# Causal mask of the first two token blocks: from one VectorE product to a ScalarE copy and a GpSimd select

## The chip, the cores and the metric

One core of a Trainium2 chip runs the whole program; the other cores do nothing. The metric is the time of one execution on the device in microseconds (us), and lower is better. Three executions of the kernel before gave 1217.30, 1218.65 and 1219.31 us, so the median is 1218.65 us.

The engines go by short names: PE is the matrix engine (PEld its weight loads), DVE is VectorE, ACT is ScalarE, POOL is GpSimd, and SP is the engine that issues most of the transfers. Each works through its own list of instructions in a fixed order.

## The reference

A gated linear recurrence (4 batches, 8 heads, 768 tokens, 48 channels) feeds two gated feed-forward layers of 3072 tokens, the second with a normalisation ahead of it:

```
a = (a_re + i a_im) * min(|a|, 0.999) / (|a| + 1e-6)
for t in range(S):
    S_state = a[t] * S_state + outer(k[t], v[t])        # complex state, 48 x 48 per head
    y[t]    = q[t] @ real(S_state)
x   = y as [3072, 384]
x   = (silu(x @ w_gate) * (x @ w_val)) @ w_out          # layer 1
out = the same with other weights on rmsnorm(x)         # layer 2
```

## The kernel before

**The recurrence** is computed in six blocks of 128 tokens. Within a block, q is multiplied by the running product of the decays and k is divided by it, so that the contribution of token p to token t is an ordinary dot product of the two. That product (`score`, PE, L699) gives for each head a 128 x 512 tile `sp` in PSUM: a row is a key token p, and the columns are four batches of 128 query tokens. Only pairs with t not before p may count. So `sp` is multiplied with a mask tile that holds -1 where t is not before p and 0 elsewhere (built once at the start, L309 to L314). The minus is there because k arrives negated from the Newton step at L653. The product (L703, DVE) writes the SBUF tile `pt`, and PE multiplies `pt` with v (`yy`, L716). From the second block on, q times the state of the earlier blocks is added (L721).

**A group** is two heads of one block, with all four batches, so there are four groups to a block and 24 in all. For each group PE transposes k and q (`trans`, L684, tile `tp`), ACT copies them to SBUF (L690 for k, L687 for q, tile `T`), PE makes the scores, DVE masks them, PE makes `yp`, and ACT copies it out (L723, tile `yt`). The update of the state (`zz`, L740, L742, then L747 to L750 on DVE) of a group is put among the instructions of the next group. What the transposes need comes from DVE and ACT: decays and their running products for two groups at a time (`e1`, L474 to L502, and `scan`), then per group a square (L618), a sum (L621), a logarithm and an exponential (L626, L627), a Newton step (L652, L653), and the products `qt` and `kt` (L646, L655, L659).

**The first layer** follows block by block: a block's feed-forward (`gv`, L360; `silu`, L369; product, L378; `acc`, L792) runs while the recurrence of the next block is computed. Its weights are split into two halves on the way in, 36 pieces in all: a transfer of 3 to 4 us, three DVE operations (L59 to L61), three ACT operations with accumulators (L330 to L332), two matmuls (`wl`, L335, L336) and another ACT copy (L337). All of that lies in the first 250 us. The second layer has no recurrence beside it.

**What sets the order.** `in_order` sorts the pieces of all tasks by due times from tables, and that is the order in which the program is written. A scheduler in the framework then orders each engine's list by priorities and its own estimates of when things are ready, so an edit in one place can move instructions elsewhere. PSUM holds two tiles under the tag `at`, which `tp`, `sp`, `yp` and `zp` share in turn; `pt` has two SBUF buffers.

**ACT's tables.** Silu needs one table of functions, logarithm and exponential share another, and each change is an instruction of its own, ACT_TABLE_LOAD. `both_logs` (L419) asks for the shared table ahead of the logarithms (L420). Where a Silu stands between that load and a logarithm, the logarithm gets a load of its own, under its own line.

Of the kernel before, what the change touches and what calls it, by code (L numbers as in the profile page):

```python
# [13 lines left out]
AF = mybir.ActivationFunctionType  # L14
ALU = mybir.AluOpType
# [3 lines left out]
B, H, S, D = 4, 8, 768, 48  # L19
# [3 lines left out]
R = 32  # L23
# [23 lines left out]
LOPE = (1, 1)  # L47
G2 = 2
NFE = G2 * D
NB = 2 * NFE // 32  # L50


LOW = 2.0 ** -15 * 1.125  # the upper word of 2^-126, read as a float


def narrow(V, raw, y):
    """float64 words -> y, the same number with float32's 24 bits."""
    lo, hi, yu = raw[:, :, 0], raw[:, :, 1], y.bitcast(U32)
    V.tensor_scalar(yu, hi, 3, 0x3FFFFFF8, op0=ALU.logical_shift_left, op1=ALU.bitwise_and)  # L59
    V.scalar_tensor_tensor(yu, hi, 0xC0000000, yu, op0=ALU.bitwise_and, op1=ALU.bitwise_or)  # L60
    V.scalar_tensor_tensor(yu, lo, 29, yu, op0=ALU.logical_shift_right, op1=ALU.bitwise_or)  # L61


def words(w, f, out_rows):
    """Block f of 128 hidden units of a weight, as [128, 768] words (or floats)."""
    k = 2 if w.dtype == U32 else 1
    if out_rows:
        return w[f * 128:f * 128 + 128, :]
    return w[:, k * f * 128:k * (f * 128 + 128)].rearrange("(c p) f -> p c f", p=128)
# [12 lines left out]


def in_order(tasks, wires):
    """The items of all tasks by the time they are due, each after those it is wired to."""
    due, after, need = {}, {}, {}
    for t, (name, (start, dur, items)) in enumerate(tasks.items()):
        total, acc = sum(c for c, _ in items), 0.0
        for n, (c, _) in enumerate(items):
            due[name, n] = (start + dur * (acc + 0.5 * c) / total, t, n)  # L90
            acc += c
            need[name, n] = 1 if n else 0
            if n:
                after.setdefault((name, n - 1), []).append((name, n))
    for a, b in wires:
        after.setdefault(a, []).append(b)
        need[b] += 1
    heap = [(due[x], x) for x in due if need[x] == 0]
    heapq.heapify(heap)
    out = []  # L100
    while heap:
        _, x = heapq.heappop(heap)
        out.append(tasks[x[0]][2][x[1]])
        for y in after.get(x, ()):
            need[y] -= 1
            if need[y] == 0:
                heapq.heappush(heap, (due[y], y))
    assert len(out) == len(due)
    return out
# [2 lines left out]
@with_exitstack  # L112
def plain_path(ctx: ExitStack, tc: tile.TileContext, q, k, v, a_re, a_im,
               wg, wv, wo, w2g, w2v, w2o, rms_g, out):
    """The recurrence step by step: for decays that a chunk's running product cannot carry."""
    nc = tc.nc
    V, A, T, SY = nc.vector, nc.scalar, nc.tensor, nc.sync
    TB, EG = 16, 4
# [6 lines left out]
    with tc.tile_pool(name="pl1", bufs=1) as p1, tc.tile_pool(name="pl2", bufs=2) as p2:  # L125
# [4 lines left out]
        with tc.For_i(0, S // TB, 1) as blk:  # L130
# [35 lines left out]
            z = [p1.tile([128, E, D], F32, name=f"pl_z{n}") for n in range(3)]  # L166
# [14 lines left out]
    with tc.tile_pool(name="pw", bufs=1) as pw, tc.tile_pool(name="px", bufs=2) as px, \  # L181
# [6 lines left out]
        for n, (g_, v_, o_) in enumerate(((wg, wv, wo), (w2g, w2v, w2o))):  # L188
# [3 lines left out]
            for f in range(NF):  # L192
                for x, t in ((g_, tg), (v_, tv), (o_, to)):
                    x = words(x, f, x is o_)
# [67 lines left out]
def decay_attention_two_ffn(ctx: ExitStack, tc: tile.TileContext, q, k, v, a_re, a_im,  # L262
# [25 lines left out]
    with ExitStack() as fast:  # L288
# [24 lines left out]
                            pattern=[[1, u], [u, R]], channel_multiplier=-1)  # L313
            masks[u] = m  # L314

# [1 line left out]
        def load_w(w, srcs, f, layer, which=(0, 1, 2)):  # L317
            for i in which:
                x = srcs[i]
# [25 lines left out]
        PAIRS = ((0, 0), (0, 1), (1, 0))  # L345

        def ffn_items(W, x, N, acc_mm, done):
            """One block of a gated layer: W[f] -> weights, x = (hi, lo) getter."""
            items = []
            st = {}  # L350

# [49 lines left out]
            items.append((0.01, done))  # L401
            return items

# [1 line left out]
        att = ExitStack()  # L405
        ap1 = att.enter_context(tc.tile_pool(name="ap1", bufs=1))
        ap2 = att.enter_context(tc.tile_pool(name="ap2", bufs=2))
# [42 lines left out]
            vt[i] = t  # L450

        def cmul(dst, t1, t2, pr, pi, z):
            """dst = (pr + i pi) * z with dst, z, t1, t2 stacked [128, 2, ...]."""
            V.tensor_tensor(t1, pr, z, op=ALU.mult)
            V.tensor_tensor(t2, pi, z, op=ALU.mult)
            V.tensor_tensor(dst[:, 0], t1[:, 0], t2[:, 1], op=ALU.subtract)
            V.tensor_tensor(dst[:, 1], t1[:, 1], t2[:, 0], op=ALU.add)

        def stack(z, like):
            """A real tile [128, ...] against a stacked one."""  # L460
            return z[:, None].to_broadcast(list(like.shape))

        def e1(p):
            """Decays of four heads, and their running products over the u tokens of a row."""
            gr = groups[2 * p]
            U, n = gr.blk.U, 2 * gr.blk.el
            s = {}
# [52 lines left out]
            return items  # L520

        def scan(p):
            """Running products over the 32 rows of a quadrant, for four heads."""
            gr = groups[2 * p]
            blk0 = gr.h0 * D // 32
            P = carry[:, :, blk0:blk0 + NB]
# [48 lines left out]
            return [(1, tr), (1.5, first), (2, pairs)] + [(2, hs(d)) for d in (1, 2, 4, 8)] + [(2, fill), (1, newcarry)]  # L575

        def back(p):
            """Products up to each row, back to tokens."""
            gr = groups[2 * p]
            U, el = gr.blk.U, gr.blk.el  # L580
            s = {}

            def go():
                x = xs[p]
                s["Xt"] = ap1.tile([128, 2, 2 * NFE], F32, tag="Xt", name="Xt", bufs=BUFS["Xt"])
                V.transpose(s["Xt"].rearrange("p c f -> p (c f)"), x[:, :, :, 0:32].rearrange("p c n r -> p (c n) r"))
                xl = an[p][:, :, U - 1]
                for c in range(2):
                    V.transpose(xl[:, c], x[:, c, :, 1:33])
                ab = ap1.tile([128, 2, 2 * NFE], F32, tag="sc1", name="ab")  # L590
                A.activation(ab, xl, AF.Abs)
                md = ap2.tile([128, 2 * G2, 2, D], F32, tag="md", name="md", bufs=BUFS["md"])
                bc = lambda z: z.rearrange("p (g d) -> p g d", d=D)[:, :, None, :].to_broadcast([128, 2 * G2, 2, D])
                V.tensor_tensor(md, bc(ab[:, 0]), bc(ab[:, 1]), op=ALU.add)
                mt[p] = md
            return s, [(3, go)]
# [76 lines left out]
        def pe_att(i):  # L673
# [21 lines left out]
            def score(h):  # L695
                def go():
# [2 lines left out]
                        T.matmul(ps[:C, bb * C:bb * C + C], o[h, 1][:, bb], o[h, 0][:, :, bb, :], start=True, stop=True)  # L699
                    t = ap2.tile([128, 512], F32, tag="pt", name="pt", bufs=BUFS["pt"])  # L700
                    m = masks[U].rearrange("p u r -> p (u r)")[:, None, :].to_broadcast([C, B, C])
                    with tc.high_priority(HP_AT):
                        V.tensor_tensor(t[:C, :N].rearrange("p (b c) -> p b c", b=B),  # L703
                                        ps[:C, :N].rearrange("p (b c) -> p b c", b=B), m, op=ALU.mult)
# [61 lines left out]
                return go  # L766
            return [(1.2, at(x)) for x in range(6)]

# [1 line left out]
        W1 = {}  # L770

        def split_x(blk):
# [84 lines left out]
        for _, fn in in_order(sch, wires):  # L857
            fn()

# [1 line left out]
        W2 = {}  # L861

        def norm(c0):
# [22 lines left out]
            return xh, xl  # L886

        def rows_of(c0, c1):
            """Columns c0:c1 of x1d as runs (partition, row of the output, length)."""
            runs = []  # L890
            for blk in blocks:
                for bb in range(B):
# [38 lines left out]
        G.memset(ones, 1.0)  # L931
        wx = fast.enter_context(tc.tile_pool(name="wx", bufs=EARLY))
        nb_ = NT // 512
        # weights of the second layer follow the last use of the first's
        def w2_loader(f):
            def go():
                W2[f] = (wx if f < EARLY else wpool).tile([128, 2, 9, 128], F32R, tag="w", name="w")
# [25 lines left out]
                    x2[n + 1] = norm(512 * (n + 1))  # L963
                fn()

# [1 line left out]
    with tc.tile_pool(name="fl", bufs=1) as fl_, tc.tile_pool(name="fps", bufs=1, space=PSUM) as fps:  # L967
        with tc.manual_schedule():
            V.tensor_scalar(stat[:, 0], stat[:, 0], 1e18, None, op0=ALU.is_le)
# [48 lines left out]
```

## Time and profile before

| what | value |
|---|---|
| median of three executions | 1218.65 us (1217.30 to 1219.31) |
| span of the profiled execution, first to last instruction | 1218.1 us (its own time is not given beyond that) |
| PE busy | 1136.6 us, 93% |
| DVE busy | 772.5 us, 63% |
| ACT busy | 668.2 us, 55% |
| POOL busy | 1.5 us, 12 instructions |
| mask products on DVE (L703) | 48, of which 16 in the first two blocks |

The busy shares are means over parts with different limits, so the windows matter more than the table. A useful ruler in this kernel is the copy of `yp` (L723), one per group: its starts cut the beginning of the run into stages. They are at 62.83, 79.37, 100.68 and 114.88 us for the four groups of the first block, and at 167.19, 195.50, 226.07 and 253.00 us for the second block. Stage 1 ends at the first of these, stage 8 at the last.

### The profile page before, as it was taken

How to read it: one execution, taken by the hardware profiler on the slowest of the kernel's cores; microseconds unless marked ns; L12 is line 12 of the kernel's file. 1: busy time of each engine (PE TensorE's matmuls, PEld its weight loads, DVE VectorE, ACT ScalarE, POOL GpSimd, SP SyncE). 2: the span in 40 equal slices, each digit the busy share in tenths (PEclk: the TensorE clock that was granted, in tenths of full speed). 3: DMA queues.
4: the chain of work that ended last, by engine and by line, in shares of the span. 5: the costliest groups of instructions: out<-in, count | busy, mean ns of one | idle time of the engine just before them, and what ended most of it. 6: DMA issues, size and time to landing. Idle time of an engine off the chain costs nothing.

```text
span 1218.1 us, 16677 instructions
## 1 busy us (share of the span) xinstructions
PE 1136.6 (93%) x6098; PEld 945.7 (78%) x6098; DVE 772.5 (63%) x1703; ACT 668.2 (55%) x1159; POOL 1.5 (0%) x12
## 2 busy tenths in 40 slices
PE   2368979999999999999999999999999999999997
PEld 1256767788888888888878887888888888888886
DVE  5997989989898696888754488742422424224222
ACT  5666979877677656675464688742421424214211
POOL 0000000000000000000000000000000000000000
PEclk9877989999999999999999999999999999999999
DMA  6355454432423224232313244400010000000000
GB/s 166 87 138 145 120 151 124 141 110 74 107 77 101 72 63 119 57 85 67 98 59 97 79 130 145 128 26 27 1 52 1 26 26 1 26 1 1 27 1 29
DMA packets 105514, 90.84 MB, mean 75 GB/s; under 512 B 34000, under 2 KB 92368, under 8 KB 105424
## 3 DMA queue, kind: packets, MB, share of 16 engines
q1 hardware_dynamic: 102832, 84.97, 24.8%
q10 hardware_dynamic: 2592, 4.72, 1.0%
q8 instruction: 50, 0.82, 0.3%
q14 instruction: 40, 0.33, 0.1%
HBM read 66.06 MB, written 18.87 MB: 70 GB/s over the span
## 4 chain that ended last, share of the span: by engine, by line
PE 72%; ACT 11%; DVE 8%; DMA 5%; issue 1%; SPq 1%; ACTq 0%; DVEq 0%
PE gv L360 39%; PE o L912 12%; PE acc L792 8%; PE sp L699 4%; PE tp L684 3%; DMA wraw<-in_moe_w_gate_dram 2%; ACT T L690 2%; PE zp L740 2%; PE yp L716 2%; DMA wraw<-in_moe_w_val_dram 2%; PE yp L721 1%; ACT w L331 1%; ACT L420 1%; ACT T L687 1%; ACT w L332 1%
## 5 line engine op out<-in xcount | busy, mean ns | idle before, releaser
L360 PE MATMUL gv<-xh,w 128*128 128x512 f32 x1728 | 571.4, 396 | 0.3 <-ACT h L369 0.3
L360 PEld LDWEIGHTS gv<-xh,w 128*128 128x128 f32 x1728 | 324.6, 188 | 68.7 <-issue 2.1
L360 PE MATMUL gv<-xl,w 128*128 128x512 f32 x864 | 339.5, 393 | 0.0
L378 DVE TENSOR_TENSOR gv<-h,gv 128x512 f32<-128x512 f32 x144 | 99.8, 693 | 225.5 <-PE gv L360 219.5
L369 ACT ACTIVATE h<-gv 128x512 f32<-128x512 f32 x144 | 85.7, 595 | 187.3 <-PE gv L360 186.8
L360 PEld LDWEIGHTS gv<-xl,w 128*128 128x128 f32 x864 | 162.6, 188 | 32.4 <-issue 1.7
L379 ACT ACTIVATE hh<-gv 128x512 fp32r<-128x512 f32 x144 | 85.5, 594 | 166.4 <-DVE gv L378 166.2
L387 DVE TENSOR_TENSOR hl<-gv,hh 128x512 fp32r<-128x512 f32 x144 | 99.1, 688 | 102.3 <-PE o L912 72.5
L792 PE MATMUL acc<-hh,w 128*128 128x512 f32 x432 | 149.0, 399 | 2.4 <-ACT hh L379 2.4
L912 PE MATMUL o<-w,hh 128*128 128x384 f32 x576 | 146.4, 336 | 0.2 <-ACT x1s L798 0.2
L912 PEld LDWEIGHTS o<-w,hh 128*128 128x128 f32 x576 | 105.6, 188 | 5.7 <-ACT x1s L798 0.5
L912 PE MATMUL o<-w,hl 128*128 128x384 f32 x288 | 96.9, 340 | 0.5 <-DVE hl L387 0.5
L792 PEld LDWEIGHTS acc<-hh,w 128*128 128x128 f32 x432 | 80.3, 188 | 21.3 <-ACT hh L379 4.3
L792 PE MATMUL acc<-hl,w 128*128 128x512 f32 x216 | 86.3, 399 | 0.7 <-DVE hl L387 0.7
L335 PE MATMUL wl<-wy,ident 128*128 128x384 f32 x72 | 39.1, 632 | 43.7 <-DVE wy L61 31.5
L690 ACT ACTIVATE T<-tp 96x512 f32<-96x512 f32 x48 | 52.6, 1097 | 43.0 <-PE tp L684 42.6
L699 PEld LDWEIGHTS sp<-T,T 96*128 96x128 f32 x384 | 51.0, 202 | 24.1 <-ACT T L687 22.6
L699 PE MATMUL sp<-T,T 96*128 96x128 f32 x384 | 56.9, 294 | 11.0 <-ACT T L687 10.7
L912 PEld LDWEIGHTS o<-w,hl 128*128 128x128 f32 x288 | 53.6, 188 | 2.6 <-DVE hl L387 2.6
L335 PEld LDWEIGHTS wl<-wy,ident 128*128 128x128 f32 x72 | 14.2, 228 | 51.8 <-DVE wy L61 36.4
L369 ACT ACT_TABLE_LOAD x38 | 48.8, 1283 | 3.4 <-PE gv L360 2.7
L792 PEld LDWEIGHTS acc<-hl,w 128*128 128x128 f32 x216 | 40.6, 188 | 11.1 <-DVE hl L387 2.8
(131 smaller groups left out, 1496.4 us busy)
## 6 DMA issues: line engine op xcount, KB each, us to landing
wraw<-in_moe_w_gate_dram SPq DMA_DIRECT2D x24, 384.0 KB, 3.5
wraw<-in_moe_w_val_dram SPq DMA_DIRECT2D x24, 384.0 KB, 3.5
wraw<-in_moe_w_out_dram SPq DMA_DIRECT2D x24, 384.0 KB, 3.1
kd<-kt SPq DMA_DIRECT2D x24, 384.0 KB, 2.6
ktok<-kd SPq DMA_DIRECT2D x24, 384.0 KB, 3.5
aar<-in_a_re_dram SPq DMA_DIRECT2D x48, 96.0 KB, 2.3
aar<-in_a_im_dram SPq DMA_DIRECT2D x48, 96.0 KB, 2.6
qk<-in_q_dram SPq DMA_DIRECT2D x96, 48.0 KB, 2.4
```

Of the source, the lines that this page charges most:

```text
L335: T.matmul(ps[:, :384], ident, y, start=True, stop=False)
L360: T.matmul(ps[:, :N], w[:, a, i + c, :], x()[b][:, c, :N], start=(n == 0), stop=(n == 8))
L369: A.activation(h[:, :N], st[f, 0][:, :N], AF.Silu)
L378: V.tensor_tensor(t[:, :N], st[f, "h"][:, :N], st[f, 3][:, :N], op=ALU.mult)
L379: A.activation(hh[:, :N], t[:, :N], AF.Copy)
L387: V.tensor_tensor(hl[:, :N], st[f, "t"][:, :N], st[f, "hh"][:, :N].bitcast(F32), op=ALU.subtract)
L684: T.transpose(ps[0:96, u * 128:u * 128 + 128], s[:, u, h].rearrange("p c d -> p (c d)"), ident)
L690: A.activation(t[:, :N].rearrange("p (b r u) -> p u b r", u=U, b=B), ps[0:96, :N].rearrange("p (u b r) -> p u b r", u=U, b=B), AF.Copy)
L699: T.matmul(ps[:C, bb * C:bb * C + C], o[h, 1][:, bb], o[h, 0][:, :, bb, :], start=True, stop=True)
L716: T.matmul(dst, vt[i][:C, col:col + 64], o[h, "p"][:C, bb * C:bb * C + C].rearrange("p (u r) -> p u r", u=U), start=True, stop=not inter)
L792: T.matmul(acc[e][:, :N], w[:, a, 6 + e, :], hs_[c][:, :N], start=(f == 0 and n == 0), stop=(f == NF - 1 and n == 2))
L912: T.matmul(acc[m][:, :DM], hs_[c][:, m * 128:m * 128 + 128], w[:, a, 6:9, :].rearrange("p c e -> p (c e)"), start=(f == 0 and x == 0), sto ...
```

## The change

For the first two blocks (`b.j < 2`, 16 of the 48 score tiles) the DVE product with the mask is not made. ACT copies the score tile out of PSUM with a factor of -1, and POOL then works in place on the SBUF tile: it keeps an element where (query token) - (key token) is not negative and writes 0 elsewhere. The other four blocks are as before. The diff also takes comments and docstrings out, so line numbers in the kernel after are one higher than before up to the score function and nine higher behind it.

```diff
+GMASK = 2
...
                     t = ap2.tile([128, 512], F32, tag="pt", name="pt", bufs=BUFS["pt"])
                     m = masks[U].rearrange("p u r -> p (u r)")[:, None, :].to_broadcast([C, B, C])
+                    if b.j < GMASK:
+                        A.activation(t[:C, :N], ps[:C, :N], AF.Copy, scale=-1.0)
+                        G.affine_select(out=t[:C, :N].rearrange("p (b u r) -> p b u r", b=B, u=U),
+                                        in_=t[:C, :N].rearrange("p (b u r) -> p b u r", b=B, u=U),
+                                        compare_op=ALU.is_ge, fill=0.0, base=0,
+                                        pattern=[[0, B], [1, U], [U, R]], channel_multiplier=-1)
+                        o[h, "p"] = t
+                        return
                     with tc.high_priority(HP_AT):
                         V.tensor_tensor(t[:C, :N].rearrange("p (b c) -> p b c", b=B),
                                         ps[:C, :N].rearrange("p (b c) -> p b c", b=B), m, op=ALU.mult)
```

The scheduler also moves other instructions. Apart from the masks, PE and SP hold the same instructions as before in another order, DVE's list has 32 products left instead of 48, POOL's has 16 selects more, and ACT's has 16 copies and seven table loads more (95 loads over the whole list, 88 before; four in each belong to the fallback path that isn't run). Counted between the copies L723, the stages 5 to 8 hold 4, 3, 4 and 3 loads before, and 5, 6, 7 and 3 after; all other stages have as many as before.

**ACT, the first group of the first block, second head.** Before, the three steps for the next group's k (L618, L626, L627) stand ahead of the copy of `yp`:

```order
L690 ACTIVATE T_418<-tp 96x4x128
L687 ACTIVATE T_445<-tp 96x512
L618 ACTIVATE e2t<-an 128x768
L626 ACTIVATE e2t<-e2t 128x384
L627 ACTIVATE e2t<-e2t 128x384
L723 ACTIVATE yt<-yp 128x512
```

The same place in the kernel after (L704 is the new copy, L732 the copy of `yp`, L619, L627 and L628 the three steps):

```order
L691 ACTIVATE T_419<-tp 96x4x128
L688 ACTIVATE T_446<-tp 96x512
L704 ACTIVATE pt<-sp 128x512
L619 ACTIVATE e2t<-an 128x768
L732 ACTIVATE yt<-yp 128x512
L627 ACTIVATE e2t<-e2t 128x384
L628 ACTIVATE e2t<-e2t 128x384
```

The new copy stands ahead of the square, and the logarithm and exponential now stand behind the copy of `yp`.

**ACT, the second group of the second block (stage 6), where the decays of two groups get their logarithm and exponential (L483, L484).** Before, the table load for them comes a few rows ahead (not shown), and the load for the Silu comes behind both:

```order
L483 ACTIVATE an<-an 128x768
L331 ACTIVATE w,wstat<-wraw 128x384
L484 ACTIVATE an<-an 128x768
L332 ACTIVATE w,wstat<-w,small 128x384
L337 ACTIVATE w<-wl 128x384
L488 ACTIVATE e1w,stat<-an 128x768
L570 ACTIVATE sc_1699<-X 128x2x6
L331 ACTIVATE w,wstat<-wraw 128x384
L369 ACT_TABLE_LOAD
L369 ACTIVATE h<-gv 128x512
```

In the kernel after:

```order
L421 ACT_TABLE_LOAD
L370 ACT_TABLE_LOAD
L370 ACTIVATE h<-gv 128x512
L484 ACT_TABLE_LOAD
L484 ACTIVATE an<-an 128x768
L380 ACTIVATE hh<-gv 128x512
L485 ACT_TABLE_LOAD
L485 ACTIVATE an<-an 128x768
L732 ACTIVATE yt<-yp 128x512
```

A Silu (L370) has moved in between the shared load and the logarithm, so that the load at L421 serves nothing, and logarithm and exponential have a load each; the copy of `yp` comes behind all four. The same pattern stands once more in the stage that follows, with L627 and L628.

**PE, between the first and the second group of the second block.** Before, the last `acc` of the piece ahead is followed at once by the transposes of the next group:

```order
L792 MATMUL acc_1060<-hh,w 128x512
L684 MATMUL tp<-ident,kt 96x128 x4
L684 MATMUL tp<-ident,qt 96x128 x3
L335 MATMUL wl<-wy,ident 128x384
L336 MATMUL wl<-w,neg 128x384
L684 MATMUL tp<-ident,qt 96x128
L360 MATMUL gv<-xh,w 128x512
L360 MATMUL gv<-xl,w 128x512
L360 MATMUL gv<-xh,w 128x512 x2
```

In the kernel after:

```order
L801 MATMUL acc_1068<-hh,w 128x512
L336 MATMUL wl<-wy,ident 128x384
L361 MATMUL gv<-xh,w 128x512
L361 MATMUL gv<-xl,w 128x512
L337 MATMUL wl<-w,neg 128x384
L361 MATMUL gv<-xh,w 128x512 x2
L361 MATMUL gv<-xl,w 128x512
L361 MATMUL gv<-xh,w 128x512 x2
L361 MATMUL gv<-xl,w 128x512
L361 MATMUL gv<-xh,w 128x512
L685 MATMUL tp<-ident,kt 96x128 x4
```

Nine matmuls of the feed-forward (one `gv` tile) and a weight piece, which in the kernel before are run ahead of the first group's `yp` or behind the transposes of the second, now stand between the two groups. Up to the end of each later group the number of `gv` matmuls is the same in both lists (126, 171 and 216 for the second to the fourth group of the second block).

## Rows read from the trace of the kernel before

**Rows 1.** The page: busy time of each engine, then DVE and ACT by slice.
```profile
PE 1136.6 (93%) x6098; PEld 945.7 (78%) x6098; DVE 772.5 (63%) x1703; ACT 668.2 (55%) x1159; POOL 1.5 (0%) x12
...
DVE  5997989989898696888754488742422424224222
ACT  5666979877677656675464688742421424214211
```
**Rows 2.** Windows by stage: length, then busy PE, PEld, DVE, ACT, POOL; PEclk; DMA.
```profile
30.00:62.83 32.83, 13.53 (x55) 9.13 (x54) 31.83 (x85) 19.87 (x41) 0.00 (x0) 0.82 0.29 85
62.83:79.37 16.54, 11.31 (x74) 9.29 (x74) 14.24 (x49) 9.17 (x19) 0.00 (x0) 0.73 0.48 131
79.37:100.68 21.31, 15.45 (x80) 10.58 (x80) 18.80 (x40) 16.29 (x39) 0.00 (x0) 0.72 0.60 166
100.68:114.88 14.20, 11.54 (x73) 9.27 (x74) 9.81 (x18) 9.87 (x21) 0.00 (x0) 0.69 0.33 96
114.88:167.19 52.31, 48.97 (x255) 38.00 (x253) 48.72 (x126) 44.88 (x101) 0.00 (x0) 1.00 0.50 140
167.19:195.50 28.31, 21.94 (x131) 17.31 (x132) 25.54 (x76) 20.87 (x40) 0.00 (x0) 0.88 0.47 129
195.50:226.07 30.57, 29.29 (x172) 22.59 (x172) 28.95 (x61) 28.33 (x59) 0.00 (x0) 1.00 0.57 164
226.07:253.00 26.93, 26.33 (x162) 20.98 (x163) 24.67 (x72) 19.70 (x33) 0.00 (x0) 1.00 0.34 93
253.00:640.00 387.00, 382.94 (x2431) 317.67 (x2430) 314.22 (x744) 252.28 (x348) 0.00 (x0) 1.00 0.31 84
```
**Rows 3.** Line L703: ns min/median/max, first and last start; DVE's idle time before it.
```profile
L703 DVE TENSOR_TENSOR pt<-sp,mask x48: 670/690/692, 55.9 to 637.2; 128x512 f32<-128x512 f32 x48
...
  PE sp L699: 20.8, 24
```
**Rows 4.** ACT's groups from 0 to 340 us: busy, mean ns, idle time before.
```profile
L420 ACT ACT_TABLE_LOAD x14 | 18.0, 1283 | 0.2
L369 ACT ACT_TABLE_LOAD x13 | 16.7, 1283 | 0.2
...
L723 ACT ACTIVATE yt<-yp 128x512 f32<-128x512 f32 x12 | 7.1, 592 | 14.9 <-PE yp L716 7.5 <-PE yp L721 7.4
```
**Rows 5.** POOL's selects over the whole run, by group.
```profile
L312 POOL TENSOR_SCALAR_AFFINE_SELECT mask<-mask 128x128 f32<-128x128 f32 x1 | 0.3, 313 | 0.0
...
L306 POOL TENSOR_SCALAR_AFFINE_SELECT small<-small 128x4 f32<-128x4 f32 x1 | 0.2, 194 | 0.0
```
**Rows 6.** ACT's timeline (start, length, idle before), first group of the first block.
```profile
56.80 0.83 ACT L618 ACTIVATE e2t<-an 128x768 f32<-128x768 f32 x1
58.26 0.52 ACT L626 ACTIVATE e2t<-e2t 128x384 f32<-128x384 f32 x1 [0.62 <-DVE e2t L621]
...
62.83 0.60 ACT L723 ACTIVATE yt<-yp 128x512 f32<-128x512 f32 x1 [3.49 <-PE yp L716]
```
**Rows 7.** DVE's timeline at the same place: what the exponential feeds.
```profile
61.80 0.55 DVE L652 TENSOR_TENSOR e2t<-e2t 128x384 f32<-128x384 f32 x1
```
**Rows 8.** ACT's timeline between the first two groups of the second block.
```profile
167.19 0.60 ACT L723 ACTIVATE yt<-yp 128x512 f32<-128x512 f32 x1 [2.46 <-PE yp L721]
167.81 1.28 ACT L420 ACT_TABLE_LOAD   x1
169.10 0.52 ACT L626 ACTIVATE e2t<-e2t 128x384 f32<-128x384 f32 x1
169.66 0.52 ACT L627 ACTIVATE e2t<-e2t 128x384 f32<-128x384 f32 x1
175.99 1.10 ACT L690 ACTIVATE T<-tp 96x512 f32<-96x512 f32 x1 [5.81 <-PE tp L684]
```
**Rows 9.** PE's timeline at the same place: the transposes that ended that wait.
```profile
174.90 1.06 PE L684 MATMUL tp<-ident,kt 128*96 128x128 f32 x4 [5.91 <-DVE X L457]
```
**Rows 10.** The chain that ended last, one piece of it.
```profile
423.23 2.08 PE gv L360 x9
```
**Rows 11.** The page, DMA issues: KB each, median us to landing.
```profile
qk<-in_q_dram SPq DMA_DIRECT2D x96, 48.0 KB, 2.4
```

## The prediction

> **What bounds the kernel now.** I read the page's busy line first: PE 93%, DVE 63%, ACT 55%, POOL 1.5 us in all [rows 1]. Over the whole span PE is the engine to beat, but the slices of DVE and ACT show that the load sits at the start: DVE is at seven to nine tenths from the second slice to the twelfth (some 365 us), and ACT is highest, at seven to nine tenths, from the fifth to the tenth [rows 1]. So I cut the start into stages at the copies of `yp` and read each stage's row [rows 2]. From 253 to 640 us PE is busy 382.94 of 387.00 us: there, a shift of the start is handed on to the end, and at most 4.06 us could be caught up. The change touches blocks 1 and 2, that is, everything up to 253 us. The time after is therefore the time before plus the shift of the last `yp` copy of block 2, as far as PE's order up to each group holds the same work, which the lists of both kernels show from stage 6 on.
>
> In stages 1 to 4 PE is far from full and DVE leads (31.83 of 32.83 us in stage 1), with ACT close in stage 3 (16.29 of 21.31). In stages 5 to 8 no engine leads alone: stage 5 has PE 48.97, DVE 48.72 and ACT 44.88 of 52.31; stage 7 has PE 29.29, DVE 28.95 and ACT 28.33 of 30.57 [rows 2]. Stage 6 has room, since PE and ACT both wait almost 6 us there for the k of the next group [rows 8, 9]. Stage 7 has none on any engine, and that decides my forecast.
>
> **The change, part by part.** The order shows that the change does what it says (16 products fewer on DVE, 16 copies and 16 selects more), so that is no rival.
>
> *Removed from DVE:* 16 products of 0.69 us, 11.0 us in all [rows 3]. DVE also stood 20.8 us idle ahead of 24 of the 48 products until the scores came; a third of it, 6.9 us, is an estimate for these 16. In two heads per stage that makes 1.4 us of work.
>
> *Added to ACT:* 16 copies of a 128 x 512 PSUM tile at 0.59 us, the price of the `yp` copy of the same shape [rows 4]: 9.5 us, 1.2 us a stage. What waits behind one in ACT's list is the list itself: weight pieces, the next group's `T` copies, the Silu. The scheduler has mostly put 1 to 3 us of other ACT work between the `T` copy and this one, so ACT seldom stops for PE's scores; the price is that `pt` comes later than the scores.
>
> *Added to POOL:* 16 selects. The trace has 0.313 us for 128 columns and 0.194 us for 4 [rows 5]. A line through both gives 0.68 us for 512 columns; four times the first gives 1.25 us. I take 0.7 us, nearer to a longer run of the same loop. POOL does nothing else, so only the path counts: from scores to `pt` it is 0.59 + 0.7 = 1.3 us (up to 1.84) in place of 0.69 us, and it is PE's `yp` that waits. From the second group on, PE has the state products, and partly feed-forward work, to do meanwhile; I put the cost of this at 0.5 us in stage 8, where in the list a table load and a Silu stand ahead of the copy, and at nothing in the others.
>
> *Table loads:* seven more, at 1.28 us [rows 4], 9.0 us in all: one in stage 5, three each in stages 6 and 7. What a load costs the chain is seen at 167.81 us: the logarithm behind it starts 1.29 us later [rows 8].
>
> The Trainium skill (ScalarE: Activation LUTs, What ACT_TABLE_LOAD costs) counts another 1.38 us of drain for each change of the set, 2.66 us together. By it seven loads would be an estimated 18.6 us. The 1.29 us from start to start does not show that drain, so the sum keeps 1.28.
>
> *Moved on SP:* the same transfers with some loads of q, k and the decays earlier or later. I cost that at nothing: the DMA engines are at most 0.60 busy in any of these stages [rows 2]. If that cover failed, one late load of q or k would cost its 2.4 us [rows 11].
>
> Now the stages.
>
> *Stages 1 to 4* (to 114.88 us). For DVE, eight products are gone, 5.5 us, against which stands an order that makes ACT later: the square at 56.80 must now wait for the second head's scores, and logarithm and exponential, which began at 58.26, come behind the `yp` copy that starts at 62.83 [rows 6]. With 0.6 us for that copy and 1.0 us for the two, the Newton step at 61.80 [rows 7] could begin at 64.4, 2.6 us later; two products fewer in DVE's queue give back 1.4. Stage 3, where ACT is loaded, gets 1.2 us. I take +1.0, with bounds of -5.5 (DVE alone decides) and +3.8 (2.6 + 1.2).
>
> *Stage 5.* DVE loses 1.4 us, and PE one `gv` tile of nine matmuls, 2.1 us [rows 10], which moves into stage 6; ACT's work is about as before (one load and two copies more, one weight piece and one Silu fewer). I take -1.5; bounds -2.1 and +1.3 (the load).
>
> *Stage 6.* ACT gets 3.85 us for the loads and 1.2 us for the copies: 20.87 + 5.0 = 25.9 of 28.31 us. It fits, since the list now puts a weight piece, a load and a Silu into the 5.81 us for which ACT sat waiting [rows 8], and PE runs its moved tile in the 5.91 us of its own wait [rows 9]. I take +0.5; bounds -2.1 and +3.
>
> *Stage 7.* ACT has 28.33 us of work in 30.57. Three loads (3.85), two copies (1.2), and one square and one more decay step against a weight step that leaves (0.8 on balance) make 34.2 us. ACT works in order, so without a single wait the stage is 3.6 us longer; with the 2.2 us for which it waited before, 5.8. I take +4.0.
>
> *Stage 8.* ACT goes from 19.70 to some 23 of 26.93 us, so PE with 26.33 stays the bound. +0.5 for the later `pt`; up to +2.
>
> The sum is 1.0 - 1.5 + 0.5 + 4.0 + 0.5 = **+4.5 us**. Against the profiled span of 1218.1 us that is 1222.6; the median lies 0.55 us above this span, and I carry that over: **1223.2 us**.
>
> **The rivals.**
>
> *A, DVE's relief decides (faster).* Place: the stages in which DVE is over 90% busy. DVE gives up 11.0 us of work and an estimated 6.9 us of waiting, and ACT's extra 18.5 us fall into its idle time, of which stages 5 to 8 hold 24.3 us and stages 1 to 4 another 30 [rows 2]. PE is idle for 11.6 us in stages 5 to 8, and more than that can't be won there; half of the 11.0 us is a fair price, -5, so 1213.6 us. It decides if the first feed-forward matmul comes earlier by more than what stage 7 loses, that is, by 4 us or more. Against it: ACT's sum for stage 7 exceeds the stage, and idle time in other stages doesn't help there.
>
> *B, a balance.* The loads fall where ACT would have waited, stage 7 loses only what stages 1 to 6 win: 1218.7 us. For it: the 5.81 us wait, and terms that differ in sign and are each of 1 to 4 us. Against it: three loads stand in stage 7 itself.
>
> *C, DVE and POOL get in each other's way (slower still).* If a select and a DVE operation with two SBUF inputs exclude each other, then 16 selects of 0.68 to 1.25 us take 10.9 to 20 us from DVE, which is all that the removed product gave, or up to 9 us more. In my sum the relief counted 2.8 us (1.4 in stages 1 to 4, 1.4 in stage 5), so 1223.2 + 2.8 = 1226.0 at the least; with half of the other 9 us on the path 1230.5. I take 1228. Nearly all of DVE's work here has two SBUF inputs. For or against it this trace has nothing: POOL is idle beside DVE [rows 1].
>
> The Trainium skill (SBUF — State Buffer, Who interferes with whom) states that rule: a DVE instruction with two SBUF inputs and a GpSimd instruction that reads SBUF share a read port, and whichever comes second waits for the whole of the other. It speaks against this change; no run here shows it yet.
>
> **How the numbers follow.** Forecast 0.50, A 0.16, B 0.18, C 0.16. A measurement of this kernel can tell about 0.2%, 2.4 us, from no change. Slower than that: the forecast without its lower edge (0.46) and C (0.16), 0.62. Same: B and that edge, 0.22. Faster: A, 0.16. The stages' bounds allow the forecast 1219 to 1230 by itself. The range reaches down to A's upper half, 1214, and up to C at its high price, 1231; it leaves out the lower half of A and the far end of C and of the forecast, some 2 in 10.
>
> **What the profile after would show.** Right: stages 6 and 7 together take some 64 us (58.9 before), with ACT over 95% busy in stage 7 and seven loads more before the last `yp` copy of block 2; the first `yp` copy within 1 us of 62.83; that of stage 8 near 257; from there on PE as full as before, and the end shifted by the same amount. DVE is less busy before 253 us, with nothing to show for it. Rival A shows in a fourth `yp` copy before 111 us; rival C in selects well over 1 us or in longer DVE operations beside them, with DVE as busy as before. My forecast is wrong if ACT's waits in stages 5 and 6 were mostly its own queue and vanish, or if scores and selects keep PE waiting for `pt` in every group, which would add up to 0.6 to 1.2 us for each of eight.

## The result, and the profile after

The kernel after takes 1226.93 us (median of five executions; four took 1225.36 to 1228.29 us, and one took 2274.63 us and stays out of every comparison), against 1218.65 before: a ratio of 1.0063, with a 95% interval of 1.0043 to 1.0084. Beside other kernels on another chip it took 1228.13 against 1218.26, 1.0085 [1.0066, 1.0104]. It is slower, by 8 to 10 us. The forecast was 1223.2 in a range of 1214 to 1231.

The page of the kernel after has this busy time of each engine (to be held against [rows 1]):

```profile
PE 1138.3 (93%) x6098; PEld 946.5 (77%) x6098; DVE 768.3 (63%) x1687; ACT 686.7 (56%) x1182; POOL 17.5 (1%) x28
```

ACT has 18.5 us more, as counted. DVE has only 4.2 us less (768.3, 772.5 before), although 16 products of 0.69 us are gone. The windows by stage, cut at the copies of `yp` (L732 here), with columns as in [rows 2]; they begin with stage 5, and the last row is the thirteenth stage, in block 4:

```profile
113.24:162.84 49.60, 46.37 (x243) 35.94 (x243) 45.34 (x115) 44.75 (x96) 1.84 (x2) 1.00 0.46 136
162.84:192.33 29.49, 25.58 (x151) 18.85 (x151) 27.59 (x81) 26.40 (x46) 1.45 (x2) 1.00 0.52 147
192.33:229.94 37.61, 31.45 (x161) 24.52 (x162) 25.82 (x51) 33.99 (x65) 1.62 (x2) 0.86 0.39 111
229.94:256.91 26.97, 26.55 (x162) 20.82 (x162) 24.91 (x72) 22.44 (x42) 1.90 (x2) 1.00 0.38 110
...
339.61:387.55 47.94, 45.77 (x244) 37.63 (x245) 37.51 (x82) 37.85 (x52) 0.00 (x0) 0.96 0.32 93
```

Against before, the copy of `yp` comes 1.6 us sooner at the end of stage 4, 4.4 sooner after stage 5, 3.2 sooner after stage 6, and 3.9 us *later* after stage 7: that stage went from 30.57 to 37.61 us. The shift stays at 3.9 us through stage 8, and then grows once more: it is 6.8 us after stage 13 and 8.1 us at the last copy. So there are two losses, one in stage 7, one in block 4, where no line of the kernel was edited.

What fills stage 7 is seen in ACT's timeline at its start (start, length):

```profile
195.27 1.28 ACT L421 ACT_TABLE_LOAD   x1
196.56 1.28 ACT L370 ACT_TABLE_LOAD   x1
197.85 0.60 ACT L370 ACTIVATE h<-gv 128x512 f32<-128x512 f32 x1
...
199.20 1.28 ACT L627 ACT_TABLE_LOAD   x1
200.49 0.52 ACT L627 ACTIVATE e2t<-e2t 128x384 f32<-128x384 f32 x1
...
201.45 1.28 ACT L628 ACT_TABLE_LOAD   x1
202.74 0.52 ACT L628 ACTIVATE e2t<-e2t 128x384 f32<-128x384 f32 x1
```

Four loads in 7.5 us, the first of them replaced before anything used it. At the same place of the kernel before, one load serves the logarithm and the exponential:

```profile
197.89 1.28 ACT L420 ACT_TABLE_LOAD   x1
199.19 0.52 ACT L626 ACTIVATE e2t<-e2t 128x384 f32<-128x384 f32 x1
...
200.03 0.51 ACT L627 ACTIVATE e2t<-e2t 128x384 f32<-128x384 f32 x1
```

PE's waits in that stage, in the kernel after, show who stood behind these loads (total, times, longest):

```profile
PE acc L801 <- ACT hh L380: 1.9, 1, 1.9
PE wl L337 <- ACT w L331: 1.7, 2, 1.1
PE tp L685 <- DVE kt L660: 1.3, 1, 1.3
PE sp L700 <- ACT T L688: 1.2, 1, 1.2
```

These are 6.1 us. Before, PE waited there once:

```profile
PE tp L684 <- DVE kt L659: 1.2, 1, 1.2
```

PE's granted clock also fell in this stage to the lower of its two levels, 1.2 instead of 2.4 GHz, twice, and both times behind such waits (before, it is 1.00 for the whole stage [rows 2]). Four windows show it, first the wait for `hh` and what followed, then the wait for `kt` and what followed (PEclk is the third number from the end):

```profile
201.92:203.80 1.88, 0.01 (x1) 0.00 (x0) 0.50 (x2) 1.87 (x4) 0.00 (x0) 1.00 0.00 0
204.50:207.50 3.00, 3.00 (x9) 2.30 (x7) 2.97 (x5) 2.97 (x9) 0.00 (x0) 0.50 0.53 160
207.90:209.22 1.32, 0.00 (x0) 0.03 (x1) 1.32 (x3) 1.32 (x5) 0.00 (x0) 1.00 0.75 174
...
211.50:217.50 6.00, 6.00 (x22) 5.01 (x23) 3.23 (x8) 4.13 (x10) 0.72 (x1) 0.50 0.60 183
```

### The profile page after: what moved, and what is told of

Read it like the earlier page. It is cut to its first block, busy times and chain, and to the rows that moved or that the text cites. A ratio compares the mean times of both kernels' runs of the same rounds, so it can differ in the third digit from the quotient of the medians.

```text
span 1226.6 us, 16728 instructions
## 1 busy us (share of the span) xinstructions
PE 1138.3 (93%) x6098; PEld 946.5 (77%) x6098; DVE 768.3 (63%) x1687; ACT 686.7 (56%) x1182; POOL 17.5 (1%) x28
## 4 chain that ended last, share of the span: by engine, by line
PE 74%; ACT 12%; DVE 7%; DMA 5%; issue 1%; SPq 0%; POOL 0%; ACTq 0%; DVEq 0%
PE gv L361 39%; PE o L921 12%; PE acc L801 8%; PE sp L700 4%; PE zp L749 2%; PE tp L685 2%; ACT T L691 2%; DMA wraw<-in_moe_w_gate_dram 2%; PE yp L725 2%; DMA wraw<-in_moe_w_val_dram 1%; PE yp L730 1%; ACT L421 1%; DMA wraw<-in_moe_w_out_dram 1%; ACT L370 1%; PE wl L336 1%
## 5 line engine op out<-in xcount | busy, mean ns | idle before, releaser
L379 DVE TENSOR_TENSOR gv<-h,gv 128x512 f32<-128x512 f32 x144 | 99.9, 694 | 229.5 <-PE gv L361 220.4
L370 ACT ACTIVATE h<-gv 128x512 f32<-128x512 f32 x144 | 85.7, 595 | 183.6 <-PE gv L361 183.2
L801 PE MATMUL acc<-hh,w 128*128 128x512 f32 x432 | 152.6, 406 | 6.5 <-ACT hh L380 6.5
L801 PEld LDWEIGHTS acc<-hl,w 128*128 128x128 f32 x216 | 41.2, 191 | 10.9 <-DVE hl L388 2.7
```

Of the source, the lines that this page charges most:

```text
L370: A.activation(h[:, :N], st[f, 0][:, :N], AF.Silu)
L379: V.tensor_tensor(t[:, :N], st[f, "h"][:, :N], st[f, 3][:, :N], op=ALU.mult)
L801: T.matmul(acc[e][:, :N], w[:, a, 6 + e, :], hs_[c][:, :N], start=(f == 0 and n == 0), stop=(f == NF - 1 and n == 2))
```

## The experiments

The theory was this: the order that the scheduler made splits the pairs of logarithm and exponential by a Silu, and the extra table loads hold up ACT in the stages where others wait for it. The rivals: the select, by its length or by a conflict with DVE, or the copy on ACT as such. The kernel before ran beside each of them on the same chip, and the ratios are to that.

### The copy on DVE, with the select kept

```diff
-                        A.activation(t[:C, :N], ps[:C, :N], AF.Copy, scale=-1.0)
+                        V.tensor_scalar(t[:C, :N], ps[:C, :N], -1.0, None, op0=ALU.mult)
```

DVE keeps 16 operations of the same length as the products, and with them all engines' lists stay almost as before (88 loads).

> In the first two blocks the negated copy out of PSUM is made by DVE in place of ACT; POOL's select stays. DVE then has as many operations as before the change, ACT none more, and the lists of all engines are those of before but for a row or two (88 table loads). What is left of the change is the select: some 0.72 us more on the way to pt, and the port that POOL may share with DVE. Theory L (the loss is ACT's table loads, which the new order brings): 1218.5 to 1221.5 us, stage 7 near 30.6 us. Rival P (the loss is the select, as a longer way to pt or as a lock against DVE): 1224 us or more.

Measured: 1220.91 us, 1.0025 [1.0014, 1.0037]; stages 5 to 8 take 52.06, 28.26, 30.41 and 26.97 us, as before. The time lies in theory L's range. With the select but with before's order, 0.25% is lost, not 0.63%: most of the loss comes with the copy on ACT and the order made around it.

### The same without the select

```diff
                         V.tensor_scalar(t[:C, :N], ps[:C, :N], -1.0, None, op0=ALU.mult)
-                        G.affine_select(out=t[:C, :N].rearrange("p (b u r) -> p b u r", b=B, u=U),
...
```

> The kernel in which DVE makes the negated copy, without the select: the scores of the first two blocks go on unmasked. All engines' lists are those of before, line by line. Against the kernel with the select this is the price of the select by itself, its way to pt and its lock with DVE. It was 3 us slower than before; theory P': all of that is the select, so this kernel is within 1 us of before, and DVE is 4 us or more less busy than with the select. Rival: the copy itself is at fault, and this one is 2 us or more above before.

Measured: 1217.24 us, 0.9993 [0.9981, 1.0005]. From this kernel to the one above, the 16 selects cost 0.32%, 3.9 us. DVE's busy time shows a conflict, since its list is the same in both; first with the select, then without:

```profile
PE 1139.9 (93%) x6098; PEld 948.5 (78%) x6098; DVE 776.6 (64%) x1703; ACT 668.8 (55%) x1159; POOL 16.8 (1%) x28
```

```profile
PE 1134.4 (93%) x6098; PEld 944.2 (78%) x6098; DVE 772.7 (64%) x1703; ACT 668.7 (55%) x1159; POOL 1.5 (0%) x12
```

The difference is 3.9 us. Counted one by one in the trace, the DVE operations that run beside a select are 4.1 us longer in all than the median of the same operations in the kernels without selects.

### One Silu, then two, held behind the exponential

A rule is added to the kernel after: a marked group's exponential is noted, and the next Silu is ordered behind it.

```diff
+PAIR = (6,)
...
-                        A.activation(h[:, :N], st[f, 0][:, :N], AF.Silu)
+                        z_ = A.activation(h[:, :N], st[f, 0][:, :N], AF.Silu)
+                    if last_exp[0] is not None:
+                        tc.add_manual_dep(z_.ins, last_exp[0].ins.name, ...)
+                        last_exp[0] = None
...
-                A.activation(s["q2"][:, 1], s["q2"][:, 1], AF.Exp, scale=-1.0)
+                x_ = A.activation(s["q2"][:, 1], s["q2"][:, 1], AF.Exp, scale=-1.0)
+                if i in PAIR:
+                    last_exp[0] = x_
```

> The changed kernel with one more rule of order: the Silu that stood between the shared table load and the logarithm of the seventh group comes behind that group's exponential. Stage 7 then has 4 table loads (7 in the changed kernel, 4 in the one before); all other stages keep their number. ACT's 16 copies and POOL's 16 selects stay. Theory L: stage 7 shrinks from 37.6 us by 3.9 us (three loads) to 7 us, and the whole to 1220 to 1223 us. Rivals P and W (W: the 16 copies themselves are too much for ACT): stage 7 stays above 36 us and the whole within 2 us of 1226.9.

Measured with `(6,)`: 1223.26 us, 1.0046 [1.0031, 1.0061]. Stages 5 to 8 hold 5, 6, 4 and 3 loads, and stage 7 is 32.28 us instead of 37.61 (34.58 in a repeat of the kernel after, below, that enters the stage 0.3 us later than this one). The whole is just above theory L's range:

```profile
194.80:227.08 32.28, 26.96 (x162) 20.87 (x161) 25.97 (x50) 30.79 (x66) 1.83 (x2) 1.00 0.46 136
```

With `PAIR = (5, 6)` the loads of stages 5 to 8 are 6, 1, 4 and 5, and 86 in all (95 in the kernel after):

> The same rule for the sixth group too. The loads in stages 5 to 8 are then 6, 1, 4, 5 (5, 6, 7, 3 in the changed kernel; 4, 3, 4, 3 before), 86 in the whole list against 95 and 88; copies and selects stay. Theory L: at or under the second kernel here, 1217 to 1221 us, stages 6 and 7 together under 61 us (67.1 in the changed kernel, 58.9 before). Rivals P and W: within 2 us of 1226.9.

Measured: 1215.91 us, 0.9985 [0.997, 1.0], 11 us under the kernel after and lower than theory L had it. Stage 6 is 26.54 us (29.49 after), stage 7 33.28:

```profile
162.52:189.06 26.54, 24.24 (x143) 18.56 (x143) 24.04 (x73) 20.27 (x45) 1.58 (x2) 0.94 0.48 142
189.06:222.34 33.28, 31.21 (x175) 24.67 (x174) 29.76 (x61) 30.81 (x65) 2.12 (x2) 0.95 0.52 151
```

The masks are still made by ACT and POOL here. So most of the loss lies in the order of the table loads and of what moves with them.

### Three loads more in the kernel before

```diff
-                    both_logs(s["i"])
+                    for _ in range(4 if i == 6 else 1):
+                        both_logs(s["i"])
```

> The kernel before, with its DVE product, and three table loads more in stage 7 alone (a Silu comes between the shared load and the seventh group's logarithm, as in the changed kernel). Theory L: stage 7 grows from 30.6 us by 2 to 5.5 us, and the whole to 1220.5 to 1224 us. Rivals P and W: the three loads fall into ACT's waits, within 1.5 us of 1218.7.

Measured: 1225.45 us, 1.0064 [1.0048, 1.0081]. Stages 5 to 8 hold 4, 3, 7 and 3 loads; stage 7 grew from 30.57 to 39.45 us, with no mask changed:

```profile
191.78:231.23 39.45, 32.66 (x172) 24.89 (x173) 28.55 (x60) 30.71 (x58) 0.00 (x0) 0.91 0.40 118
```

With three extra loads (3.85 us) the stage is 8.9 us longer, and stage and whole are beyond what theory L had. ACT is idle for 8.7 us of the stage, where it was 2.2 us before, so its work alone doesn't make the difference. Part of it is that the Silu which now stands ahead of the logarithm waits for PE, and all behind it wait too:

```profile
198.40 1.28 ACT L369 ACT_TABLE_LOAD   x1 [2.95 <-PE gv L360]
```

The clock was lower for part of the stage as well (0.91). PE's order moved too, in this stage and later, so loads, waits and order can't be told apart here.

### The rule in the kernel before

> The kernel before with the same rule of order for the sixth and seventh groups (a Silu comes behind their exponentials), and no change of the mask. The loads in stages 5 to 8 are 3, 4, 4, 3 (4, 3, 4, 3 before), 88 in all as before. If the mask change is worth something once the loads are paired, this kernel stays at the time of before (within 1.5 us) and 1.5 us or more above the changed kernel with the rule for both groups. If the rule alone made that kernel fast, this one is as fast, 1215 to 1216.5 us.

Measured with `PAIR = (5, 6)` in the kernel before: 1221.43 us, 1.0033 [1.0014, 1.0052]. That is 3.7 us above the kernel before, where at most 1.5 were expected; stage 5 takes 54.73 us (52.31 before) and stage 7 32.02 (30.57), and the reason is open. The rule by itself is no gain, so what it gave above is the repair of an order that the mask change had spoiled.

### Holding back a Silu in block 4 too

> The changed kernel with the rule for the sixth, seventh and fourteenth groups: stages 12 to 14 (block 4) then have 1, 6, 2 loads (2, 9, 2 in the changed kernel; 2, 8, 3 before). Theory L for the second loss (stages 12 to 14 took 4.6 us more in the changed kernel than before): they come down by 2 to 4 us, and the whole is 1.5 to 4 us under the kernel with the rule for two groups. Rival: that loss is PE's changed order, not ACT's loads, and the time stays within 1 us of that kernel.

> The kernel before with the rule for the fourteenth group alone: stages 12 to 14 have 1, 5, 2 loads (2, 8, 3 before), and nothing changes in the first two blocks. Theory L: stage 13 has 45.55 of 45.66 us of PE work in the kernel before, so loads cost nothing there and the time stays within 1.5 us of before. If it falls by 2 us or more, loads in block 4 are on the path in the old kernel too, and the rule is a gain by itself.

With `PAIR = (5, 6, 13)` in the kernel after: 1236.92 us, 1.0158 [1.0145, 1.0172], with two loads fewer than `(5, 6)`. With `PAIR = (13,)` in the kernel before: 1238.70 us, 1.0179 [1.0165, 1.0192], with five loads fewer than before. Both expectations were far off. In both the thirteenth stage is some 20 us longer; its window, and PE's longest wait in it, in the first of the two:

```profile
328.88:397.16 68.28, 53.45 (x261) 43.66 (x262) 45.92 (x95) 37.68 (x54) 0.00 (x0) 0.83 0.26 75
```

```profile
PE tp L692 <- DVE kt L667: 11.7, 1, 11.7
```

In ACT's list the Silus of the feed-forward now stand behind the logarithms and exponentials of two groups, so PE has no feed-forward work while it waits for the next `kt`, 11.7 us in one piece, and its clock is at 0.83 over the stage. The number of loads decides nothing by itself; what counts is who is kept waiting behind them, and here fewer loads were bought with a starved PE.

### The select taken out of the kernel with both Silus held, and repeats

Three kernels on one chip: that with `PAIR = (5, 6)` without its selects, the kernel after once more, and `PAIR = (5, 6)` once more.

> The kernel with both groups' Silus held back (sixth and seventh group), without the sixteen selects: scores of the first two blocks stay unmasked. Its lists differ from that kernel's in the first eight stages (87 table loads instead of 86), and are the same behind them. Theory: a select costs what it cost between the kernel with DVE's copy and the one without selects, some 3.9 us over the run, through the longer way to pt and through DVE instructions held up beside it: 1212 us, DVE 3 to 5 us less busy than 770. Rival: with the copy on ACT the scores wait in ACT's list anyhow, so the select is hidden and the time stays within 1.5 us of 1216. DVE busy decides on the lock by itself, whatever the time does.

> The kernel after once more, beside the others of this call. It tells how much of the 4.6 us that its first trace lost between the eleventh and fourteenth copy of yp belongs to the program. Theory: the program (another order of block 4's pieces): thirteenth stage again 47 to 49 us against 45.7, last yp copy again 7 to 9 us later than before's, time 1226 to 1228. Rival: an accident of one profiled execution: thirteenth stage near 45.7, last copy some 4 us late.

> The kernel with both groups' Silus held back once more, beside the kernel after and the kernel before. Expected 1214 to 1217 us, a ratio to before of 0.997 to 1.000; the stage that ends with the seventh yp copy 32 to 34 us against some 37.6 in the kernel after, and the sixth 26 to 27. The rival, that its first result was luck, would give 1218 to 1222.

| kernel | us | ratio to before |
|---|---|---|
| before | 1218.26 | |
| Silus held, no select | 1212.77 | 0.9948 [0.9931, 0.9966] |
| Silus held | 1216.98 | 0.9986 [0.9976, 0.9996] |
| after | 1228.13 | 1.0085 [1.0066, 1.0104] |

Read downwards, this is a ladder: 16 products off DVE and onto ACT are worth -5.5 us where the loads don't suffer; the selects cost +4.2; the order that the scheduler made without the rule costs +11.2. The first step has the rule in it, whose own share is not measured (in the kernel before it cost 3.7 us). In the second step DVE's busy time goes from 765.0 to 770.5 us (768.4 in the earlier run of the same kernel); counted one by one, the operations beside selects are stretched by 4.2 us (2.4 in the earlier run).

In the repeat of the kernel after, stage 7 and stage 13 were:

```profile
195.11:229.69 34.58, 28.33 (x161) 22.13 (x162) 25.34 (x51) 33.71 (x66) 1.71 (x2) 0.95 0.44 122
...
339.32:387.15 47.83, 45.66 (x244) 37.66 (x244) 37.48 (x82) 37.85 (x51) 0.00 (x0) 0.96 0.33 93
```

The second loss is there again: from the eighth copy of `yp` to the last it takes 391.1 us (391.6 in the first trace, 387.4 before), so it belongs to the program. Stage 7, however, ended at the same time (229.69 and 229.94 us) though it began 2.8 us later: in the first trace PE was slow for longer (clock 0.86, not 0.95; busy 31.45, not 28.33 us), and the early start was lost. Two traces of one program differ by up to 2.6 us at the end of the first block (113.24 and 115.84 here), so a stage sum of one trace is good to about that.

## Why the prediction was right, and where it was not

**The direction, and place and mechanism of the loss in stage 7, held.** The forecast said that stage 7 has no room on ACT and that three more loads there decide. In stage 7 ACT was to have 34.2 us of work; it had 33.99 and 33.71, which is 97% of the stage in the repeat, where over 95% was named, and 90% in the first trace. Taking the split of the seventh group's pair away gave 5.3 us of stage 7 against the first trace and 2.3 us against the repeat, and with three extra loads in the kernel before the same stage was longer with no mask changed. Of the signs named, the first `yp` copy came at 61.25 us (within 1 us of 62.83 was asked; it was 1.6 sooner, and 1.2 in the repeat), that of stage 8 at 256.91 and 256.65 (near 257), and stages 6 and 7 took 67.1 and 64.1 us together (64).

**Term by term**, shift in us, forecast against the first trace and the repeat:

| stages | forecast | first trace | repeat |
|---|---|---|---|
| 1 to 4 | +1.0 | -1.6 | +1.0 |
| 5 | -1.5 | -2.7 | -2.5 |
| 6 | +0.5 | +1.2 | +1.2 |
| 7 | +4.0 | +7.0 | +4.0 |
| 8 | +0.5 | 0.0 | 0.0 |
| sum at the eighth copy | +4.5 | +3.9 | +3.7 |
| behind it | 0 | +4.2 | +3.7 |

Up to the eighth copy the sum was right to 1 us, though in part because larger terms cancelled: there the ladder of kernels above reads -7.5, +4.2 and +7.0 us (253.00, 245.50, 249.67, 256.65), so relief, selects and order each weighed more than in the sum. Stage 5 gained more than its -1.5, even beyond its bound of -2.1; the later `pt` in stage 8 cost nothing. Stage 7's +4.0 took ACT's work without the waits; in the first trace the waits and the low clock came on top (7.0, beyond the bound of 5.8), and swallowed what the stages up to 6 had gained. The bounds of the stages, added up, run from -5.6 to +15.9 us, 1213 to 1235 us; the 1219 to 1230 that the forecast allowed itself is narrower, and it doesn't say why.

**The step that failed** is the hand-on: "a shift of the start is handed on to the end". It was argued from PE's busy share after 253 us and from PE's list, and ACT's list in block 4 was not read. (The text on the change even says that outside stages 5 to 8 the loads are as many as before. That is wrong: stages 13 and 14 hold 9 and 2 after, 8 and 3 before.) In block 4 both loads and order have changed. A pair is split in the same way as in stage 7; first ACT's timeline of the kernel before, then of the kernel after:

```profile
345.31 0.60 ACT L369 ACTIVATE h<-gv 128x512 f32<-128x512 f32 x1
345.93 1.28 ACT L420 ACT_TABLE_LOAD   x1
347.23 0.53 ACT L626 ACTIVATE e2t<-e2t 128x384 f32<-128x384 f32 x1
...
348.39 0.51 ACT L627 ACTIVATE e2t<-e2t 128x384 f32<-128x384 f32 x1
```

```profile
348.67 1.28 ACT L421 ACT_TABLE_LOAD   x1
349.96 0.53 ACT L627 ACTIVATE e2t<-e2t 128x384 f32<-128x384 f32 x1
...
351.80 0.60 ACT L370 ACTIVATE h<-gv 128x512 f32<-128x512 f32 x1
...
353.71 0.53 ACT L628 ACTIVATE e2t<-e2t 128x384 f32<-128x384 f32 x1
```

The Silu that stood ahead of the load now stands between logarithm and exponential, and the exponential comes 5.0 us after the load where it came 2.5 us after it. PE does not wait at this place, though. It waits once in the whole stage, more than 10 us later; in the kernel before it waits nowhere in it:

```profile
PE acc L801 <- ACT hh L380: 2.2, 1, 2.2
```

Between the eighth copy and the last, PE stands idle for 6.0 us (391.59 less 385.62 busy), 1.9 us more than before (387.39 less 383.33). It is also busy 2.3 us longer; some 1.7 us of that are the clock, which is at its lower level for 3.4 us just behind that wait:

```profile
364.48:366.65 2.17, 0.00 (x1) 0.00 (x0) 0.68 (x3) 2.16 (x4) 0.00 (x0) 1.00 0.80 198
368.50:371.50 3.00, 3.00 (x8) 2.33 (x8) 3.00 (x6) 3.00 (x6) 0.00 (x0) 0.50 0.02 7
```

What this wait hangs on can be read from the rows ahead of it. The product that `hh` needs (L379, DVE) is done at 363.61 us, but `hh` stands behind a copy (`xh`), a table load and a logarithm, and that copy could not start until PE was through a row of `gv` matmuls:

```profile
362.92 0.69 DVE L379 TENSOR_TENSOR gv<-h,gv 128x512 f32<-128x512 f32 x1
363.64 0.63 ACT L786 ACTIVATE xh<-xf 128x512 fp32r<-128x512 f32 x1 [0.63 <-PE gv L361]
364.30 1.28 ACT L421 ACT_TABLE_LOAD   x1
365.59 0.52 ACT L627 ACTIVATE e2t<-e2t 128x384 f32<-128x384 f32 x1
366.02 0.58 ACT L380 ACTIVATE hh<-gv 128x512 fp32r<-128x512 f32 x1
```

In the kernel before, the `hh` beside the same logarithm starts 0.4 us after its product (done at 360.29), and the copies of `xh` come behind it:

```profile
359.59 0.70 DVE L378 TENSOR_TENSOR gv<-h,gv 128x512 f32<-128x512 f32 x1
360.69 0.58 ACT L379 ACTIVATE hh<-gv 128x512 fp32r<-128x512 f32 x1
...
361.58 1.66 ACT L777 ACTIVATE xh<-xf 128x512 fp32r<-128x512 f32 x3
```

The kernel with `PAIR = (6,)` has the same wait of 2.2 us without the fall of the clock, is busy 383.94 us there, and lost 2.3 us instead of 4.2. All three traces with this list in block 4 (the kernel after twice, and the one with `PAIR = (6,)`, 389.7 us) have the `xh` copy ahead of the load, have the wait and lose time here; those with the copy on DVE and with `PAIR = (5, 6)`, where that copy stands behind `hh` and the earlier pair stands together, take 387.5 and 386.5 us. So the wait goes back to the order of ACT's list, with a load in it again, but to a place behind the split pair. That the split pair has a part in it is not shown: no run changed the one without the other, and the one attempt to mend block 4 alone moved too much.

**Rival A (DVE's relief) was real and lost.** Its price of -5 us is close to what the kernel with Silus held and no select shows (-5.5, with the rule in it). In the kernel after it is overruled by the loads, as the forecast argued, and by the select; its sign, a fourth copy of `yp` before 111 us, did not come (113.24 and 115.84).

**Rival C (DVE and POOL in each other's way) was real, at a third to half of its size at most.** It counted 10.9 to 20 us taken from DVE; the busy times of kernels with and without selects differ by 3 to 6 us. In the kernel after, counted one by one, the operations beside selects are longer by 2.5 us (1.5 in the repeat); the rest of what is missing from the relief there has another source, for even without selects DVE's busy time falls by 7.5 us (772.5 to 765.0) and not by 11.0. In the kernel's time the selects cost 3.9 and 4.2 us in two pairs of kernels. The forecast put that at 0.5 us. How much of it is the conflict and how much the longer way to `pt` is not separated. That the measured time lies close to C's 1228 does not make C the cause, for with the selects still there `PAIR = (5, 6)` runs at 1216 to 1217.

Two places in the trace of the kernel after show the conflict from both sides. The longest select, 3.50 us where the median is 0.73, stands beside eight DVE operations that run back to back at their usual lengths, from 53.90 to 56.83 us (the first and the last are shown), and ends 0.6 us after them. Later a DVE operation takes 1.06 instead of 0.55 us beside a select (106.97 and 106.42 us). POOL's rows come first, then DVE's:

```profile
53.92 3.50 POOL L705 TENSOR_SCALAR_AFFINE_SELECT pt<-pt 128x512 f32<-128x512 f32 x1 [51.96 <-ACT pt L704]
...
106.42 1.22 POOL L705 TENSOR_SCALAR_AFFINE_SELECT pt<-pt 128x512 f32<-128x512 f32 x1 [8.37 <-ACT pt L704]
```

```profile
53.90 0.35 DVE L457 TENSOR_TENSOR an<-sc,sc 128x192 f32<-128x192 f32 x1
...
56.48 0.35 DVE L458 TENSOR_TENSOR an<-sc,sc 128x192 f32<-128x192 f32 x1
...
106.97 1.06 DVE L455 TENSOR_TENSOR sc<-an 128x384 f32<-128x384 f32 x1
```

The Trainium skill (SBUF — State Buffer, Who interferes with whom) calls the shared port an exclusive lock, by which whichever instruction comes second waits for the whole of the other. These rows agree that each side can be held up; the 3.50 us select shows that POOL can be held up past several DVE operations in a row.

**Rival B (a balance)** fell with the +11 us that the order costs.

**Table loads.** The Trainium skill (ScalarE: Activation LUTs, What ACT_TABLE_LOAD costs) has 2.66 us for a change of set, drain included. Here each load again takes 1.28 us and the instruction behind it starts 1.29 us after it (195.27 to 196.56, 199.20 to 200.49), so no drain shows, and ACT's sum of stage 7 came out with 1.28.

## What to carry to other kernels

When an edit shifts an engine's list, read that list to the end of the program, not only where the edit is: a Silu that slips between a table load and its two users costs loads and keeps everybody behind ACT waiting, and in block 4, far from the edit, a copy that slipped ahead of a load cost a wait too. Work moved from a busy engine was worth something here only where such pairs stayed together: with two Silus held back the same change went from a ratio of 1.0085 to one of 0.9986. And count who waits, not how many loads: two kernels with fewer loads lost 20 us, because PE had nothing to do while the pairs stood together.

## What the runs showed of the hardware that was not expected

- A select of 128 x 512 on POOL takes 0.726 us in the median, beside the 0.68 us of the line through the two shorter ones [rows 5]; single ones took 3.50 us (3.55 in the repeat, 4.43 with Silus held) while DVE was working without a pause.
- With three extra table loads of 1.28 us each a stage without room became 8.9 us longer, more than twice their own 3.85 us, with 8.7 us in which ACT was idle and with the granted clock of PE at 0.91 instead of 1.00. Three loads fewer in the kernel after gave 5.3 or 2.3 us, by which of its two traces they are held against.
- The same program, twice: stage 7 took 37.61 and 34.58 us and ended 0.25 us apart, with the clock at 0.86 and 0.95. The early start of the first was lost within that stage.
